# Transposing the normalised activations by DMA instead of on TensorE, and folding the rms weights into the normalisation

## Chip, core and metric

The kernel runs on one core of one Trainium2 chip. The metric is device time in microseconds of one launch. The profile is one profiled execution of the same program; its times count from the first instruction.

## What is computed

Attention with a cluster mask, followed by a gated feed-forward network (FFN), in float32 at the borders:

```python
batch, n_heads, seq, head_dim = (4, 8, 768, 64);  n_clusters = 16
n_tokens, d_model, d_ff = (3072, 512, 1536)

mask = q_assign[:, :, :, None] == k_assign[:, :, None, :]   # nearest centroid of q and of k
scores = np.where(mask, scale * np.matmul(q, k.transpose(0, 1, 3, 2)), -1e9)
attn = softmax(scores)
x = np.matmul(attn, v)        # heads side by side: 3072 x 512
rms = np.sqrt(np.mean(x * x, axis=-1, keepdims=True) + 1e-06)
xn = x / rms * rms_g
g = xn @ w_gate
val = xn @ w_val
out = (silu(g) * val) @ w_out
```

## The kernel before

**Units.** The 3072 tokens are cut into 8 units of 384 (three tiles of 128 tokens: `HT = 3`), two for each batch. For a unit, `scores` (L323) computes the masked scores of one head, with the cluster one-hot rows appended to q and k, and ScalarE takes their exponential from PSUM; `pv` (L341) multiplies by v and puts the head's normalised result into x, 128 tokens by 512 features per tile.

**From x to the FFN.** `squares` (L366) sums the squares of x; `rms` (L378) forms the inverse root with small VectorE operations and multiplies each of the three tiles by it (L386), giving xn in bf16, tokens on partitions. The FFN's matmuls contract over features, so they need xnT, features on partitions: four blocks of 128 features by 384 tokens. `xtrans` (L390) makes one such block: three TensorE transposes of 128x128 against `ident` into a PSUM tile "tx", then one VectorE instruction that multiplies by `gcol` (the rms weights, one column per block, so one scalar per partition) and writes xnT. For unit 0, `xtrans_all` (L399) does all four blocks together, with one of the four evictions on ScalarE. `gv` (L415) takes xnT as the moving operand: four matmuls for one block of 128 gate or value columns; ScalarE and VectorE make gvT of them. `out_mm` (L444) multiplies gvT by the output weights, 36 matmuls a unit in nine pieces; ScalarE copies the result to SBUF and SP stores it.

**Order.** The program is written out by hand under a manual schedule: engines work in program order, and waits follow from the tiles. `attention` (L636) goes through the 24 score steps of a unit (8 heads by 3) and puts pieces of other work behind each of them, as far as their listed costs ask. While the scores of unit u are computed, the pieces are: the last eight gate and value blocks of unit u-2, then `rms(u-1)`, then `out_mm` of unit u-2, then the first 16 gate and value blocks of unit u-1, with the preparation of a later group of heads spread among these. `CUT` marks where a unit's FFN is split between two such stretches. `border` (L532) puts the four `xtrans` of unit u-1 between the last pieces of `out_mm`. Unit 1's stretch is different: `norm` is called after the second score step (`rms(0)`, and the casts of four heads on GpSimd behind it), `xtrans_all(0)` after the sixth (`LEAD = 6`), and the first gate of unit 0 follows the seventh. After unit 7's scores come the rest of unit 6's FFN, `rms(7)`, and then unit 6's output and unit 7's FFN with nothing else between.

**Queues and buffers.** SP issues the loads of q, k and v, each waiting for a free staging buffer, and the output stores, all in program order. GpSimd issues the weight loads, which convert to bf16. x has two buffers, xn and xnT one each: xnT of a unit can be written once the unit before has had its last value matmul. The FFN's PSUM tiles, "tx" among them, rotate through three buffers. The SBUF tiles "th" of the gate pool rotate through three as well.

**The start.** `c_in`, `c_sq`, `c_n`, `ones`, `cnt` and `cntT` are small constants used in the first microseconds to build the identity and the normalised centroids; each has a place of its own. `gcol` is loaded by SP after the first loads (L569).

Of the kernel before, what the change touches and what calls it, by code (L numbers as in the profile page):

```python
# [9 lines left out]
F32 = mybir.dt.float32  # L10
BF16 = mybir.dt.bfloat16
I32 = mybir.dt.int32
AX = mybir.AxisListType.X
ALU = mybir.AluOpType
ACT = mybir.ActivationFunctionType
# [7 lines left out]
def kernel(  # L23
# [12 lines left out]
    nc = tc.nc  # L36
    B, H, S, D = q.shape
    NC = centroids.shape[1]
    DM = moe_w_gate.shape[0]
    DF = moe_w_gate.shape[1]  # L40
    P = 128
    ST = S // P
    HT = ST // 2
    UQ = HT * P
    HG = 4
    NG = B * H // HG
    UNITS = [(b, c, HT) for b in range(B) for c in (0, HT)]
    NU = len(UNITS)
    CC = DM // P
    FC = DF // P  # L50
    scale = 1.0 / (D ** 0.5)
    KR = D + NC
    WARM = 7
    CUT = CC + 2 * FC - 8
    LEAD = 6
    NQ, NV = 6, 8

# [2 lines left out]
    const = pool("const", 1)  # L60
# [4 lines left out]
    xp = pool("xp", 1)  # L65
    small = pool("small", 3)
    gate = pool("gate", 3)
# [3 lines left out]
    ps_g = pool("ps_g", 3, space=PSUM)  # L71
# [8 lines left out]
    def load(n, part, on=None):  # L80
        if n not in staged:
            staged[n] = stage.tile([P, 2, ST, D], F32, tag="qk", name="qk")
        (on or nc.sync).dma_start(out=staged[n][:, part], in_=src((q, k)[part], n))
# [9 lines left out]
        stagedv[n] = stage.tile([P, ST, D], F32, tag="vs", name="vs", bufs=NV)  # L93
        (vq or nc.sync).dma_start(out=stagedv[n], in_=src(v, n))

    c_in = const.tile([P, D], F32)
    nc.sync.dma_start(out=c_in, in_=centroids.rearrange("h c d -> (h c) d"))
    load(0, 0)
    load(0, 1, nc.scalar)
# [2 lines left out]
    for n in range(2, NQ):  # L102
        load(n, 1)
        load(n, 0)
    gcol = const.tile([P, CC], F32)


    qext = [const.tile([P, HG, S], BF16, name=f"qext{i}") for i in range(4)]
# [30 lines left out]
        return y2  # L139


    ones = const.tile([P, 32], F32)
    nc.vector.memset(ones, 1.0)
    cnt = const.tile([P, 32], F32)
    nc.vector.tensor_tensor_scan(cnt, ones, ones, 0.0, op0=ALU.mult, op1=ALU.add)
    cntT = const.tile([P, 32], F32)
    nc.vector.transpose(cntT, cnt)
    ident_f = const.tile([P, P], F32)
    nc.vector.memset(ident_f, 0.0)
    for i in range(P // 32):  # L150
        r = slice(32 * i, 32 * i + 32)
        nc.vector.tensor_tensor(ident_f[r, r], cnt[r, :], cntT[r, :], op=ALU.is_equal)
    ident = const.tile([P, P], BF16)
    nc.vector.tensor_copy(ident, ident_f)


    vbf = [const.tile([P, HG, ST, D + 1], BF16, name=f"vbf{i}") for i in range(4)]
# [5 lines left out]

    cblk = const.tile([P, H, 2 * NC], F32)
    nc.gpsimd.memset(cblk, 0.0)
    c_sq = const.tile([P, D], F32)
    c_ss = const.tile([P, 1], F32)
    nc.vector.tensor_mul(c_sq, c_in, c_in)
    nc.vector.reduce_sum(c_ss, c_sq, axis=AX)
# [3 lines left out]
    nc.scalar.activation(first_exp, off, ACT.Exp)  # L173
    c_inv = const.tile([P, 1], F32)
    nc.vector.reciprocal(c_inv, c_norm)
    c_n = const.tile([P, 2 * D], F32)
    nc.vector.tensor_scalar_mul(c_n[:, :D], c_in, c_inv)
    nc.vector.tensor_scalar_mul(c_n[:, D:], c_in, c_inv)

# [182 lines left out]
    xn = {}  # L362
# [15 lines left out]
    def rms(u):  # L378
        x, nt = xs[u], UNITS[u][2]
        for t in range(nt):  # L380
            squares(u, t, True)
        ms = small.tile([P, HT], F32, tag="ms", name="ms")
        nc.vector.scalar_tensor_tensor(ms[:, :nt], sq[u][:, 0, :nt], 1e-6, sq[u][:, 1, :nt], op0=ALU.add, op1=ALU.add)
        y = rsqrt(ms[:, :nt], nt)
        for t in range(nt):
            nc.vector.tensor_scalar_mul(xn[u][:, t], x[:, t], y[:, t:t + 1])  # L386

    xnT, gvT = {}, {}

    def xtrans(u, c):  # L390
        if c == 0:
            xnT[u] = xp.tile([P, CC, UQ], BF16, tag="xnT", name="xnT")
        ps = ps_g.tile([P, UQ], BF16, tag="gen", name="tx")
        w = UNITS[u][2] * P
        for t in range(UNITS[u][2]):
            nc.tensor.transpose(ps[:, t * P:(t + 1) * P], xn[u][:, t, c * P:(c + 1) * P], ident)  # L396
        nc.vector.tensor_scalar_mul(xnT[u][:, c, :w], ps[:, :w], gcol[:, c:c + 1])  # L397

    def xtrans_all(u):  # L399

        xnT[u] = xp.tile([P, CC, UQ], BF16, tag="xnT", name="xnT")
        ps = [ps_g.tile([P, 2, UQ], BF16, tag="gen", name="tx") for _ in range(3)]
        to = [ps[(c + 1) // 2][:, (c + 1) % 2] for c in range(CC)]
        for t in range(HT):
            for c in range(CC):
                nc.tensor.transpose(to[c][:, t * P:(t + 1) * P], xn[u][:, t, c * P:(c + 1) * P], ident)
        for c in range(CC):
            if c < CC - 1:
                nc.vector.tensor_scalar_mul(xnT[u][:, c], to[c], gcol[:, c:c + 1])
            else:  # L410
                nc.scalar.activation(xnT[u][:, c], to[c], ACT.Copy, scale=gcol[:, c:c + 1])

    gates = {}

# [29 lines left out]
    def out_mm(u, t, part):  # L444
        if part == 0:
            outs[u] = ps_g.tile([P, DM], F32, tag="gen", name="o")
        for f in range(4 * part, 4 * part + 4):
            nc.tensor.matmul(outs[u], lhsT=gvT[u][:, f, t * P:(t + 1) * P], rhs=wo[:, f], start=f == 0, stop=f == FC - 1)  # L448
        if part == 2:
            o = outp.tile([P, DM], F32, tag="o_sb", name="o_sb")  # L450
            nc.scalar.copy(o, outs[u])  # L451
            nc.sync.dma_start(out=out_rows(u, t), in_=o)
# [52 lines left out]
    def group(g):  # L505
        t, c, a = group_work(g)
        return [x for h in range(HG) for x in t[2 * h:2 * h + 2] + c[2 * h:2 * h + 2]] + a

    def spread(a, b):

        if not a:
            return list(b)
        w, n = [], 0
        for i, x in enumerate(a):
            w.append(x)
            while n < len(b) * (i + 1) // len(a):
                w.append(b[n])
                n += 1
        return w

    def ffn_work(u):
        n = UNITS[u][2] / HT
        w = [(0.18 * n, lambda c=c: xtrans(u, c)) for c in range(CC)]
        for f in range(FC):
            for val in (False, True):
                w.append((0.64 * n, lambda f=f, val=val: gv(u, f, val)))
        return w

    def out_work(u):
        return [(0.86, lambda t=t, p=p: out_mm(u, t, p)) for t in range(UNITS[u][2]) for p in range(3)]  # L530

    def border(o, ffn):  # L532

        return o[:-2] + ffn[:2] + o[-2:-1] + ffn[2:4] + o[-1:]


    def tokens(g, h, on=None):
        trans(g, h, 1, on)
# [27 lines left out]
        load_v(n)  # L566
    for n in range(H, H + HG):
        load_qk(n)
    nc.sync.dma_start(out=gcol, in_=moe_rms_g.rearrange("(c p) -> p c", p=P), allow_slow_non_contiguous=True)  # L569
    tokens(0, 2)  # L570
    casts(pool_, 2, K0, K1, Q0)
    pair_clusters(0, (1,))
# [63 lines left out]
    def attention(heads, fill, skip=0, hooks={}):  # L636
        gaps = [(u, h, i) for u, h in heads for i in range(UNITS[u][2])]
        total, done, n = sum(c for c, _ in fill), 0.0, 0
        for at, (u, h, i) in enumerate(gaps):
            scores(u, h, i)  # L640
            if i == (0 if (u, h) == (1, 0) else 1):
                for p in due:
                    pv(*p)
                due[:] = [(u, h)]
            if h == H - 1:
                squares(u, i, False)
            if (u, h, i) in hooks:
                hooks[u, h, i]()
            while n < len(fill) and at >= skip and done <= total * (at + 1 - skip) / (len(gaps) - skip):
                done += fill[n][0]  # L650
                fill[n][1]()
                n += 1
        for _, f in fill[n:]:
            f()

    attention([(0, h) for h in range(H)], [], hooks={(0, *divmod(i, HT)): f for i in range(H * HT) for f in [first.get(i, more)] if f})
    for u in range(1, NU):
        ffn, o, g = ffn_work(u - 1), out_work(u - 2) if u > 1 else [], u + 2
        if u == 1:
            t, c, a = group_work(2)  # L660
            t3, c3, a3 = group_work(3)
            n = LEAD - 4
            o3 = [(0.0, lambda i=i: load_o(i)) for i in range(0, FC, 4)]
            prep = c + a + spread(weave(t3[n:], c3), o3) + a3[:5]
            idle = const.tile([P, 1], BF16)

            def norm():
                rms(0)
                nc.gpsimd.tensor_copy(idle, xn[0][:, HT - 1, DM - 1:])
                for h in range(HG):  # L670
                    casts(pool_, H + h, K0, Q0, K1, Q1)

            hooks = {(1, 0, 0): late[6], (1, 0, 1): lambda: (late[7](), norm())}
            hooks.update({(1, *divmod(2 + i, HT)): t3[i][1] for i in range(n)})
            hooks[1, *divmod(LEAD - 1, HT)] = lambda: xtrans_all(0)
            fill = spread(ffn[CC:CUT], prep)
            attention([(1, h) for h in range(H)], fill, LEAD, hooks)
        else:
            fill = ffn_work(u - 2)[CUT:] + [(0.0, lambda u=u: rms(u - 1))]
            fill += border(spread(o[:3], [(0.0, f) for _, f in a3[5:]]) + o[3:], ffn) if u == 2 else border(o, ffn)  # L680
            attention([(u, h) for h in range(H)], fill + spread(ffn[CC:CUT], group(g) if g < NG else []), 1 if g < NG else 0)
    rest = ffn_work(NU - 2)[CUT:]
    rest[0][1]()
    pv(NU - 1, H - 1)
# [1 line left out]
        f()  # L686
    rms(NU - 1)
    nc.scalar.activation(first_exp, off, ACT.Silu)
    for _, f in border(out_work(NU - 2), ffn_work(NU - 1)) + ffn_work(NU - 1)[CC:] + out_work(NU - 1)[:-3]:
        f()  # L690
    for i in range(3):
        out_part(NU - 1, HT - 1, i)
# [30 lines left out]
```

The softmax here doesn't subtract the row's maximum and nothing guards it: scores larger than these inputs give would overflow.

## Time and profile before

| | |
|---|---|
| time, three runs | 345.44 us median (345.31 to 345.99) |
| span of the profiled execution | 343.6 us |
| median of the runs less the span | 1.84 us |
| granted TensorE clock | 1.000 |
| DMA traffic | 31.62 MB, mean 92 GB/s |
| SP load of q, 192 KB, issue to landing | median 3.9 us, 32 loads |
| SP output store, 256 KB, issue to landing | median 2.0 us, 23 stores |

The span is the time between the first and the last recorded instruction; the profile gives no other time for that execution, so the difference to the median of the runs stands for what lies around it. In the profile's rows PE is TensorE's matmul stream, PEld its weight loads, DVE VectorE, ACT ScalarE, POOL GpSimd, SP the engine that issues most DMAs; a "q" after the name is the engine's queue. A row of groups gives the line, engine, operation, output and inputs, shapes and count, then busy time and mean duration in ns, then idle time of the engine ahead of it and what ended it.

### The profile page before, as it was taken

The page shows a single profiled execution, that of the slowest core. Times are in us where ns is not written, and L with a number is a line of the kernel's source. Part 1 is how long each engine was busy: PE and PEld are TensorE (multiplying, and loading weights), DVE is VectorE, ACT ScalarE, POOL GpSimd, SP SyncE. Part 2 cuts the span into 40 slices and gives each one's busy share as a digit, 9 for nine tenths or more (in the row PEclk, how much of TensorE's full clock was granted, in tenths as well). Part 3 has the DMA queues.
Part 4 walks back from the last instruction along what each step waited for, and adds up shares of the span by engine and source line. Part 5 has one row for each costly group of instructions (what it writes and reads, how often), then busy time and mean ns, then how long its engine had stood idle before and what let it go on. Part 6 is the DMA issues. An engine that isn't in the chain of part 4 may idle for free.

```text
span 343.6 us, 8003 instructions
## 1 busy us (share of the span) xinstructions
PE 336.0 (98%) x3045; PEld 208.2 (61%) x3045; DVE 219.9 (64%) x540; ACT 259.7 (76%) x449; POOL 112.9 (33%) x225
## 2 busy tenths in 40 slices
PE   8999999999999999999999999999999999999996
PEld 3547657555766567665675656756566656655654
DVE  6999796975577626785367745686455635575330
ACT  5899979856979768786797777888688877763322
POOL 6999596234335305271131801516000000000000
PEclk9999999999999999999999999999999999999999
DMA  8999989882450015401130011000100011001002
GB/s 276 384 210 216 248 166 237 134 267 97 149 158 14 31 62 152 139 18 40 61 94 2 23 53 41 2 5 21 63 32 0 2 46 49 2 1 64 31 2 92
DMA packets 27302, 31.62 MB, mean 92 GB/s; under 512 B 4480, under 2 KB 24320, under 8 KB 27264
## 3 DMA queue, kind: packets, MB, share of 16 engines
q1 hardware_dynamic: 18608, 25.02, 22.2%
q0 software_dynamic: 8368, 5.71, 10.4%
q8 instruction: 24, 0.39, 0.5%
q10 hardware_dynamic: 288, 0.39, 0.4%
q14 instruction: 14, 0.11, 0.1%
HBM read 28.35 MB, written 6.29 MB: 101 GB/s over the span
## 4 chain that ended last, share of the span: by engine, by line
PE 82%; ACT 9%; DVE 6%; DMA 1%; issue 1%; DVEq 0%; ACTq 0%
PE o L448 17%; PE val L423 16%; PE gate L423 16%; PE s L333 15%; PE acc L351 9%; ACT pT L337 6%; PE tq L208 4%; PE sc L241 3%; PE tx L396 1%; ACT xn L376 1%; ACT th L431 1%; DVE pads L312 1%; DVE kext L317 1%; DVE qext L317 1%; DMA c_in<-in_centroids_dram 1%
## 5 line engine op out<-in xcount | busy, mean ns | idle before, releaser
L337 ACT ACTIVATE pT<-s,off 128x768 bf16<-128x768 f32 x192 | 171.3, 905 | 39.7 <-PE s L333 38.7
L333 PE MATMUL s<-qext,kext 80*128 80x384 bf16 x384 | 94.8, 327 | 2.4 <-ACT pT L337 1.6
L432 DVE SCALAR_TENSOR_TENSOR th<-th,gate 128x384 f32<-128x384 f32 x84 | 46.4, 552 | 50.8 <-ACT th L431 50.6
L423 PE MATMUL gate<-xnT,wg 128*128 128x384 bf16 x384 | 78.5, 325 | 0.1
L423 PE MATMUL val<-xnT,wv 128*128 128x384 bf16 x384 | 78.1, 326 | 0.1
L448 PE MATMUL o<-wo,gvT 128*128 128x512 bf16 x276 | 67.6, 379 | 0.0
L227 POOL CAST qext<-qkT 64x384 bf16<-64x384 f32 x64 | 35.3, 558 | 72.3 <-ACT qkT L214 63.8
L333 PEld LDWEIGHTS <-kext 80*128 80x128 bf16 x384 | 36.4, 98 | 35.1 <-issue 9.9
L436 DVE SCALAR_TENSOR_TENSOR gvT<-th,val 128x384 bf16<-128x384 f32 x84 | 46.3, 551 | 6.8 <-PE val L423 2.0
L423 PEld LDWEIGHTS <-wv 128*128 128x128 bf16 x384 | 36.3, 97 | 22.4 <-issue 0.7
L423 PEld LDWEIGHTS <-wg 128*128 128x128 bf16 x384 | 36.2, 97 | 22.0 <-issue 0.8
L351 PEld LDWEIGHTS <-pT 128*128 128x128 bf16 x1152 | 43.4, 97 | 10.1 <-DVE x L358 1.0
L431 ACT ACTIVATE th<-gate 128x384 f32<-128x384 f32 x84 | 41.3, 492 | 9.4 <-PE gate L423 8.8
L351 PE MATMUL acc<-vbf,pT 128*128 128x65 bf16 x1152 | 45.7, 193 | 0.6 <-ACT pT L337 0.2
L448 PEld LDWEIGHTS <-gvT 128*128 128x128 bf16 x276 | 25.6, 97 | 25.2 <-issue 0.6
L208 PE MATMUL tq<-ident_f,qk 128*128 128x128 f32 x192 | 30.9, 276 | 0.0
L282 POOL DMA_DIRECT2D qext<-oh x40 | 19.1, 486 | 34.7 <-DVE oh L271 28.3
L214 ACT ACTIVATE qkT<-tq 128x384 f32<-128x384 f32 x57 | 27.4, 494 | 3.4 <-PE tq L208 2.9
L397 DVE TENSOR_SCALAR xnT<-tx,gcol 128x384 bf16<-128x384 bf16 x28 | 10.4, 412 | 27.5 <-PE tx L396 27.5
L208 PEld LDWEIGHTS tq<-ident_f,qk 128*128 128x128 f32 x192 | 23.2, 141 | 6.6 <-ACT qkT L214 1.0
L451 ACT COPY o_sb<-o 128x512 f32<-128x512 f32 x23 | 13.5, 586 | 15.5 <-PE o L448 15.5
L282 POOL DMA_DIRECT2D kext<-oh x40 | 19.1, 485 | 9.6 <-DVE oh L271 9.6
(81 smaller groups left out, 246.2 us busy)
## 6 DMA issues: line engine op xcount, KB each, us to landing
qk<-in_q_dram SPq DMA_DIRECT2D x32, 192.0 KB, 3.9
vs<-in_v_dram SPq DMA_DIRECT2D x32, 192.0 KB, 4.2
out_dram<-o_sb SPq DMA_DIRECT2D x23, 256.0 KB, 2.0
qk<-in_k_dram SPq DMA_DIRECT2D x30, 192.0 KB, 3.9
wg<-in_moe_w_gate_dram POOLq DMA_DIRECT2D x4, 384.0 KB, 8.7
wv<-in_moe_w_val_dram POOLq DMA_DIRECT2D x4, 384.0 KB, 11.0
wo<-in_moe_w_out_dram POOLq DMA_DIRECT2D x3, 512.0 KB, 8.9
qext<-oh POOLq DMA_DIRECT2D x40, 12.0 KB, 1.6
```

The costliest lines, as they stand in the source:

```text
L208: nc.tensor.transpose(ps[:, i * P:(i + 1) * P], qk[:, part, 2 * i:2 * i + 2].rearrange("p t d -> p (t d)"), ident_f)
L214: nc.scalar.activation(to, ps, ACT.Copy, scale=by)
L227: on.tensor_copy(to, of)
L282: on.dma_start(out=ext[D:D + NC, h, e * UQ:(e + 1) * UQ], in_=put[g, m][32 * h + e * NC:32 * h + (e + 1) * NC])
L333: nc.tensor.matmul(ps[:, j, :w] if nt == HT else flat[:, j * w:(j + 1) * w], lhsT=cols(kext[g % 4][:KR, hh], g, kc // HT, kc % HT * P, (kc ...
L337: nc.scalar.activation(pT[u, h][:, n * i:n * i + n, :w], of, ACT.Exp, bias=off, scale=scale * ZS)
L351: nc.tensor.matmul(acc[:, h % 2, t], lhsT=pT[u, h][:, kc, t * P:(t + 1) * P], rhs=vbf[g % 4][:, hh, kc % HT * 2 + kc // HT], start=kc == 0 ...
L423: nc.tensor.matmul(ps, lhsT=w[:, c, f * P:(f + 1) * P], rhs=xnT[u][:, c, :n], start=c == 0, stop=c == CC - 1)
L431: nc.scalar.activation(th, ps, ACT.Tanh, scale=0.5)
L432: nc.vector.scalar_tensor_tensor(th, th, 1.0, ps, op0=ALU.add, op1=ALU.mult)
L436: nc.vector.scalar_tensor_tensor(gvT[u][:, f, :n], gates[u], 0.5, ps, op0=ALU.mult, op1=ALU.mult)
L448: nc.tensor.matmul(outs[u], lhsT=gvT[u][:, f, t * P:(t + 1) * P], rhs=wo[:, f], start=f == 0, stop=f == FC - 1)
```

## The change

The normalisation multiplies by the rms weights too: `grow` holds them as a row of 512 on all partitions and is the third operand. Behind the three normalisations, `rms` now calls `xtrans`, which issues three DMA transposes on SP, each from one tile of xn (128 tokens by 512 features) to the 128 token columns of all four blocks of xnT. The TensorE transposes, their PSUM tiles and evictions, `xtrans_all`, `border`, `gcol` and the bf16 identity are gone. `CUT` is four less, since the FFN's list no longer begins with four transposes; the same gate and value blocks fall on either side of it. The six small constants of the start share one buffer of the gate pool, `boot`.

```diff
-    c_in = const.tile([P, D], F32)
+    boot = gate.tile([P, UQ], F32, tag="th", name="boot")
+    c_in, c_sq, c_n = boot[:, :D], boot[:, D:2 * D], boot[:, 2 * D:4 * D]
+    ones, cnt, cntT = [boot[:, 4 * D + 32 * i:4 * D + 32 * i + 32] for i in range(3)]
...
-    gcol = const.tile([P, CC], F32)
+    grow = const.tile([P, DM], F32)
...
-    ident = const.tile([P, P], BF16)
-    nc.vector.tensor_copy(ident, ident_f)
...
         for t in range(nt):
-            nc.vector.tensor_scalar_mul(xn[u][:, t], x[:, t], y[:, t:t + 1])
+            nc.vector.scalar_tensor_tensor(xn[u][:, t], x[:, t], y[:, t:t + 1], grow, op0=ALU.mult, op1=ALU.mult)
+        xtrans(u)
...
-    def xtrans(u, c):
-        if c == 0:
-            xnT[u] = xp.tile([P, CC, UQ], BF16, tag="xnT", name="xnT")
-        ps = ps_g.tile([P, UQ], BF16, tag="gen", name="tx")
-        w = UNITS[u][2] * P
+    def xtrans(u):
+        xnT[u] = xp.tile([P, CC, UQ], BF16, tag="xnT", name="xnT")
         for t in range(UNITS[u][2]):
-            nc.tensor.transpose(ps[:, t * P:(t + 1) * P], xn[u][:, t, c * P:(c + 1) * P], ident)
-        nc.vector.tensor_scalar_mul(xnT[u][:, c, :w], ps[:, :w], gcol[:, c:c + 1])
+            nc.sync.dma_start_transpose(out=xnT[u][:, :, t * P:(t + 1) * P], in_=xn[u][:, t])
...
-        w = [(0.18 * n, lambda c=c: xtrans(u, c)) for c in range(CC)]
+        w = []
...
-    nc.sync.dma_start(out=gcol, in_=moe_rms_g.rearrange("(c p) -> p c", p=P), allow_slow_non_contiguous=True)
+    nc.sync.dma_start(out=grow, in_=moe_rms_g.unsqueeze(0).broadcast_to([P, DM]))
...
-            hooks[1, *divmod(LEAD - 1, HT)] = lambda: xtrans_all(0)
-            fill = spread(ffn[CC:CUT], prep)
+            fill = spread(ffn[:CUT], prep)
...
-            fill += border(spread(o[:3], [(0.0, f) for _, f in a3[5:]]) + o[3:], ffn) if u == 2 else border(o, ffn)
+            fill += spread(o[:3], [(0.0, f) for _, f in a3[5:]]) + o[3:] if u == 2 else o
...
-    for _, f in border(out_work(NU - 2), ffn_work(NU - 1)) + ffn_work(NU - 1)[CC:] + out_work(NU - 1)[:-3]:
+    for _, f in out_work(NU - 2) + ffn_work(NU - 1) + out_work(NU - 1)[:-3]:
```

More of the change, by code (lines that the diff above doesn't have):

```diff
@@ L53 @@
     WARM = 7
-    CUT = CC + 2 * FC - 8
+    CUT = 2 * FC - 8
     LEAD = 6
@@ L139, in rsqrt @@
         return y2
-    ones = const.tile([P, 32], F32)
     nc.vector.memset(ones, 1.0)
-    cnt = const.tile([P, 32], F32)
     nc.vector.tensor_tensor_scan(cnt, ones, ones, 0.0, op0=ALU.mult, op1=ALU.add)
-    cntT = const.tile([P, 32], F32)
     nc.vector.transpose(cntT, cnt)
@@ L165 @@
     nc.gpsimd.memset(cblk, 0.0)
-    c_sq = const.tile([P, D], F32)
     c_ss = const.tile([P, 1], F32)
@@ L175 @@
     nc.vector.reciprocal(c_inv, c_norm)
-    c_n = const.tile([P, 2 * D], F32)
     nc.vector.tensor_scalar_mul(c_n[:, :D], c_in, c_inv)
@@ L385, in rms @@
         for t in range(nt):
-            nc.vector.tensor_scalar_mul(xn[u][:, t], x[:, t], y[:, t:t + 1])
+            nc.vector.scalar_tensor_tensor(xn[u][:, t], x[:, t], y[:, t:t + 1], grow, op0=ALU.mult, op1=ALU.mult)
+        xtrans(u)
     xnT, gvT = {}, {}
-    def xtrans(u, c):
-        if c == 0:
-            xnT[u] = xp.tile([P, CC, UQ], BF16, tag="xnT", name="xnT")
-        ps = ps_g.tile([P, UQ], BF16, tag="gen", name="tx")
-        w = UNITS[u][2] * P
-        for t in range(UNITS[u][2]):
[L396 to L411, printed above, removed]
+    def xtrans(u):
+        xnT[u] = xp.tile([P, CC, UQ], BF16, tag="xnT", name="xnT")
+        for t in range(UNITS[u][2]):
+            nc.sync.dma_start_transpose(out=xnT[u][:, :, t * P:(t + 1) * P], in_=xn[u][:, t])
     gates = {}
@@ L530, in out_work @@
         return [(0.86, lambda t=t, p=p: out_mm(u, t, p)) for t in range(UNITS[u][2]) for p in range(3)]
-    def border(o, ffn):
-        return o[:-2] + ffn[:2] + o[-2:-1] + ffn[2:4] + o[-1:]
     def tokens(g, h, on=None):
@@ L679 @@
             fill = ffn_work(u - 2)[CUT:] + [(0.0, lambda u=u: rms(u - 1))]
-            fill += border(spread(o[:3], [(0.0, f) for _, f in a3[5:]]) + o[3:], ffn) if u == 2 else border(o, ffn)
-            attention([(u, h) for h in range(H)], fill + spread(ffn[CC:CUT], group(g) if g < NG else []), 1 if g < NG else 0)
+            fill += spread(o[:3], [(0.0, f) for _, f in a3[5:]]) + o[3:] if u == 2 else o
+            attention([(u, h) for h in range(H)], fill + spread(ffn[:CUT], group(g) if g < NG else []), 1 if g < NG else 0)
     rest = ffn_work(NU - 2)[CUT:]
```

## Prediction

> **What bounds the kernel now.** I read the page's busy shares first, then the chain that ended last.
>
> ```profile
> PE 336.0 (98%) x3045; PEld 208.2 (61%) x3045; DVE 219.9 (64%) x540; ACT 259.7 (76%) x449; POOL 112.9 (33%) x225
> PE 82%; ACT 9%; DVE 6%; DMA 1%; issue 1%; DVEq 0%; ACTq 0%
> ```
>
> TensorE is busy nearly always and carries 82% of the chain. A busy PE need not be at its peak, so I ask for the stretches around the change (length, then each engine's busy time and count; clock, DMA share and GB/s last), and then who PE waits for:
>
> ```profile
> 38.00:44.00 6.00, 5.87 (x71) 3.66 (x71) 3.87 (x10) 5.47 (x9) 4.46 (x11) 1.00 1.20 271
> 86.00:105.00 19.00, 19.00 (x191) 12.83 (x190) 12.01 (x28) 16.08 (x29) 6.07 (x12) 1.00 0.45 140
> PE s L333 <- ACT pT L337: 1.6, 6, 0.3
> ```
>
> From about 40 us PE has no holes: its largest wait, summed over the run, is 1.6 us. So a microsecond of PE work taken out after 40 us is a microsecond won, and a microsecond for which the in-order PE stands still is lost with nothing later to absorb it. The second thing to see is the 1.20 beside 38 to 44 us: the DMA engines are full there, with loads of v and weights.
>
> The transposes themselves, by tile and by form:
>
> ```profile
> L396 PE MATMUL tx<-ident,xn x84: 217/219/222, 83.0 to 316.1; 128*128 128x128 bf16 x84
> L397 DVE TENSOR_SCALAR xnT<-tx,gcol 128x384 bf16<-128x384 bf16 x28 | 10.4, 412 | 27.5 <-PE tx L396 27.5
> L386 DVE TENSOR_SCALAR xn<-x,n 128x512 bf16<-128x512 f32 x24 | 10.2, 483 | 0.3
> ```
>
> Last, the timeline at three unit borders (units 0, 2 and 7): from the normalisation to the first gate matmul, which needs all of xnT.
>
> ```profile
> 37.89 1.28 DVE L386 TENSOR_SCALAR xn<-x,n 128x512 bf16<-128x512 f32 x3
> 40.15 1.24 PE L423 MATMUL gate<-xnT,wg 128*128 128x384 bf16 x4
> ...
> 119.07 1.28 DVE L386 TENSOR_SCALAR xn<-x,n 128x512 bf16<-128x512 f32 x3
> 127.13 0.81 PE L423 MATMUL gate<-xnT,wg 128*128 128x384 bf16 x4
> ...
> 311.47 1.28 DVE L386 TENSOR_SCALAR xn<-x,n 128x512 bf16<-128x512 f32 x3
> 316.98 0.81 PE L423 MATMUL gate<-xnT,wg 128*128 128x384 bf16 x4
> ```
>
> The windows are 2.3, 8.1 and 5.5 us. Units 3 and 4 are as unit 2; unit 1 has 9.3, units 5 and 6 have 8.9 (the same two rows there).
>
> [...] the later of SP's loads at 35 us take 8 us and more to land where the median is 3.9. [...] the first warm matmuls (L117, 512 columns) start 0.43 us apart, the later o matmuls of that width 0.216.
>
> **The change part by part.**
>
> *PE.* 96 transposes go. In a run they advance PE by 0.34 us per six on the chain (84 of them, 14 groups: 4.76 us), and the first unit's twelve by 0.67. Together 5.4 us, all on the path. The gate could then start 0.67 us earlier at each border.
>
> *DVE and ACT.* Away go 31 evictions of 0.41 us, one ACT eviction of 0.65 and the 0.73 us ident cast. The 24 normalisations take a second SBUF tensor, grow. The nearest row is x<-acc,inv, a two-tensor op at 557 ns for 384 columns; with 128 more at its slope (557/384) about 0.7 us against 0.48, bounds 0.6 and 0.9 (L373, also two-tensor, reached 0.91 beside POOL). DVE has net 8 us less work and isn't the bound: nothing either way. Each first slice is ready 0.7 us after its normalisation starts, the third after some 1.9.
>
> *The start.* The six small constants in one gate buffer touch separate columns, and the buffer is rewritten only at the third gate: nothing, at worst 1 us if the engines were held for c_in's landing (2.4 us). grow is 256 KB read where gcol was 2 KB in 4-byte pieces that took 9.2 us to land; one load of its size, needed 20 us later. Its cost lies under the loads of that stage: nothing.
>
> *The new transfers.* Each unit issues three on SP, each waiting for its slice and for the last val matmul of the unit before (done before the normalisation). How far apart they run is the unknown. [...] The lower bound is 0.5 us, since a plain 192 KB load occupies SP for 0.33 to 0.43; [...] I take 1.4[...]. Landing after the last issue: 2.0 us, as the output stores. So xnT is complete 0.7 + 3 x 1.4 + 2.0 = 6.9 us after the normalisation starts, where the rings are free.
>
> *Units 1 to 6.* The first gate is due (window less the 0.67) at 8.6, 7.4 (three times) and 8.2 (twice). 6.9 is under each: hidden under out_work, by only 0.5 us at units 2 to 4. Behind the waiting transfers on SP stand three output stores, which lose up to 5 us; their buffers (three) are next wanted a unit later, so nobody waits.
>
> *Unit 7.* Due at 316.3; landing at 311.47 + 6.9 = 318.4. PE stands 2.1 us. [...]
>
> *Unit 0.* The gate is due at 40.15 - 0.67 = 39.5. SP reaches the transfers in time (its v loads are out by 35.7, and the q and k loads of head 14 and the blocked v load now come after). But these rows show what is ahead of them in the rings:
>
> ```profile
> vs<-in_v_dram SPq DMA_DIRECT2D x2, 192.0 KB, 8.4
> wg<-in_moe_w_gate_dram POOLq DMA_DIRECT2D x1, 384.0 KB, 12.2
> wv<-in_moe_w_val_dram POOLq DMA_DIRECT2D x1, 384.0 KB, 13.3
> qk<-in_q_dram SPq DMA_DIRECT2D x1, 192.0 KB, 8.6
> qk<-in_k_dram SPq DMA_DIRECT2D x1, 192.0 KB, 8.9
> ```
>
> The last q and k load (issued 35.77 and 36.48) landed at 44.4 and 45.4. The three transposes are as many bytes and take that place behind the v loads: 45.4, and an estimated 1.1 more for smaller pieces interleaved with the weights, 46.5. Even on free rings 38.6 + 4.2 + 2.0 = 44.8. PE stands 7.0 us; bounds 2.8 (pitch 0.5, no queue) and 11 (the weights' share doubling their time). No other PE work can slip in, since the gate stands in PE's order. [...]
>
> *Sum.* -5.4 + 7.0 + 1.7 + 2.1 = +5.4. On the profiled span of 343.6 that is 349.0; the median of the runs stands 1.84 above the span, so 350.8.
>
> **The rivals.**
>
> *A, slow transfers.* A pitch of 2.6 us [...] brings xnT after 10.5 us: stalls of 1.9 at unit 1, 3.1 three times, 2.3 twice, 5.7 at unit 7, 9 at unit 0, and cold clocks at 0 and 7 (3.4): 33.9 less 5.4, so 373.9. [...] Against: 128 KB is less than a load that lands in 2.3 us on free rings.
>
> *B, all hidden but little.* Pitch 0.5 and no queue at unit 0: stall 2.8 there, none elsewhere, no cold clock: 345.44 - 5.4 + 2.8 = 342.8. It wins where unit 0's stall stays under 5.4. Against it: the 8 to 9 us landings. A middle of A to B lands within the noise.
>
> *C, a coarse dependence at the start* (boot held as one piece) would add its 1 us to the forecast: 351.8, inside its range.
>
> **How the numbers follow.** The forecast, 346.5 to 357 with its bounds (stall at unit 0 of 4 to 11, at unit 7 of 0 to 5): 0.60. A: 0.24. B: 0.12. Even: 0.04. A run tells changes over 0.2% (0.7 us) from none. Faster 0.12, same 0.04, slower 0.84. The range 344 to 374 leaves out most of B and the upper third of A, 0.19.
>
> **What would show it.** PE's idle time before gate L423: some 7 us near 39.5, 2 us near 316, next to none at the six others. SP's transposes 1.4 us apart, landing about 8 us after issue near 40 us and 2 later. Gate matmuls at twice their spacing for some 3 us after the first stall. No tx rows; L386's successor near 0.7 us. The prediction is wrong if units 2 to 4 wait too (pitch above 1.6), or if the first stall is under 5 us.

## The result, and the profile after

The changed kernel takes 353.79 us (median of four runs, 352.84 to 354.62) against 345.47 us: 1.0235 of the time before, 95% interval 1.0215 to 1.0255, so slower by 8.3 us. The profiled spans, 352.0 and 343.6 us, differ by 8.4, so the account below is made on the spans.

First the page of the changed kernel: busy shares, chain, and the granted clock in 40 slices of 8.8 us.

```profile
PE 333.2 (95%) x2949; PEld 203.7 (58%) x2949; DVE 216.3 (61%) x508; ACT 259.5 (74%) x448; POOL 112.3 (32%) x225
PEclk9999959999999999999999999999999999999999
PE 77%; POOL 7%; DMA 6%; ACT 5%; issue 2%; DVE 2%; SPq 1%; ACTq 0%; DVEq 0%; POOLq 0%
```

PE has 96 matmuls fewer and is busy for a smaller share; DMA and GpSimd have come into the chain; one clock slice, the sixth (44 to 53 us), is low. Who PE waits for (total in us, times, longest) names the place:

```profile
PE gate L401 <- DMA xnT<-xn: 10.6, 2, 9.6
PE s L328 <- ACT pT L332: 2.3, 7, 0.7
```

Two of eight units wait for their transposed tile. PE's timeline at the first of them (unit 0) and at the other (unit 7):

```profile
40.61 0.50 PE L328 MATMUL s<-qext,kext 80*128 80x384 bf16 x2 [0.67 <-ACT pT L332]
50.69 1.44 PE L401 MATMUL gate<-xnT,wg 128*128 128x384 bf16 x4 [9.58 <-DMA xnT<-xn]
51.92 1.48 PE L401 MATMUL val<-xnT,wv 128*128 128x384 bf16 x4
...
325.38 0.81 PE L401 MATMUL gate<-xnT,wg 128*128 128x384 bf16 x4 [1.06 <-DMA xnT<-xn]
```

Four gate matmuls that took 0.81 us at the last unit take 1.44 at the first: after 9.58 idle microseconds PE runs at half clock (0.50). Two stretches (length, five engines' busy time and count, clock, DMA share, GB/s) show the stall, in which nothing but GpSimd and the DMA engines works, and the half clock behind it:

```profile
44.00:47.50 3.50, 0.00 (x0) 0.00 (x0) 0.00 (x0) 0.00 (x0) 3.28 (x8) 0.50 1.29 192
51.00:54.00 3.00, 3.00 (x13) 1.43 (x12) 1.11 (x2) 0.49 (x1) 2.11 (x4) 0.50 0.97 297
```

What the half clock cost against the kernel before is read from unit 0's second gate block, before and after:

```profile
42.77 0.81 PE L423 MATMUL gate<-xnT,wg 128*128 128x384 bf16 x4
...
54.46 0.81 PE L401 MATMUL gate<-xnT,wg 128*128 128x384 bf16 x4
```

From the first gate matmul to this one it is 2.62 us before (from 40.15) and 3.77 after (from 50.69), so about 1.2 lost. Against steps at full clock and without holes the loss would be 1.6 (the gate, value and score steps behind the stall take 3.2 us from start to start instead of 1.6), but the first gate block of the kernel before is slow too, 1.24 us.

The account: +9.6 at unit 0, +1.2 for the half clock, +1.1 at unit 7, -5.4 for the transposes that are gone: +6.5. Another 0.8 came in before 11 us; the kernel before has part of that too when it is profiled again (below). Another 0.7 is the wait in the first of the timeline's rows: the score step at 40.61 waits 0.67 us for ScalarE, where before unit 0's twelve transposes filled PE's time. Those 0.67 us of the 5.4 were not won. That makes 8.0 of the 8.4; the rest lies at units 1 to 7, where PE's order shows some 4.5 us won by the transposes that are gone, not 4.8, and 1.2 lost at unit 7's border, not 1.1.

### The profile page after: what moved, and what is told of

Its sections match the earlier page's. It is cut to its first block, busy times and chain, and to the rows that moved or that the text cites. A ratio compares the mean times of both kernels' runs of the same rounds, so it can differ in the third digit from the quotient of the medians.

```text
span 352.0 us, 7867 instructions
## 1 busy us (share of the span) xinstructions
PE 333.2 (95%) x2949; PEld 203.7 (58%) x2949; DVE 216.3 (61%) x508; ACT 259.5 (74%) x448; POOL 112.3 (32%) x225
## 4 chain that ended last, share of the span: by engine, by line
PE 77%; POOL 7%; DMA 6%; ACT 5%; issue 2%; DVE 2%; SPq 1%; ACTq 0%; DVEq 0%; POOLq 0%
PE o L426 16%; PE val L401 16%; PE gate L401 16%; PE s L328 14%; PE acc L346 8%; PE tq L203 4%; DMA xnT<-xn 3%; PE sc L236 3%; POOL kext L222 2%; POOL qext L222 2%; ACT pT L332 2%; DMA vs<-in_v_dram 2%; ACT xn L371 1%; ACT th L409 1%; POOL vbf L225 1%
## 5 line engine op out<-in xcount | busy, mean ns | idle before, releaser
L328 PEld LDWEIGHTS <-kext 80*128 80x128 bf16 x384 | 36.6, 99 | 36.2 <-issue 11.1
L401 PEld LDWEIGHTS <-wv 128*128 128x128 bf16 x384 | 36.7, 98 | 22.8 <-issue 1.2
L346 PEld LDWEIGHTS <-pT 128*128 128x128 bf16 x1152 | 43.5, 97 | 10.2 <-DVE x L353 1.0
L353 DVE TENSOR_TENSOR x<-acc,inv 128x384 f32<-128x384 f32 x32 | 17.8, 557 | 1.1
```

Source lines behind the costliest of these rows:

```text
L328: nc.tensor.matmul(ps[:, j, :w] if nt == HT else flat[:, j * w:(j + 1) * w], lhsT=cols(kext[g % 4][:KR, hh], g, kc // HT, kc % HT * P, (kc ...
L346: nc.tensor.matmul(acc[:, h % 2, t], lhsT=pT[u, h][:, kc, t * P:(t + 1) * P], rhs=vbf[g % 4][:, hh, kc % HT * 2 + kc // HT], start=kc == 0 ...
L401: nc.tensor.matmul(ps, lhsT=w[:, c, f * P:(f + 1) * P], rhs=xnT[u][:, c, :n], start=c == 0, stop=c == CC - 1)
```

## Experiments

Each is the changed kernel with one edit unless said otherwise.

### Unit 0, then units 0 and 7, transposed on TensorE

The normalisation still multiplies by the row, so the evictions are plain copies; `border` puts unit 7's four blocks between the output pieces.

```diff
         for t in range(nt):
             nc.vector.scalar_tensor_tensor(xn[u][:, t], x[:, t], y[:, t:t + 1], grow, op0=ALU.mult, op1=ALU.mult)
-        xtrans(u)
+        if u not in ON_PE:          # {0}, then {0, 7}
+            xtrans(u)
...
+            hooks[1, *divmod(LEAD - 1, HT)] = lambda: xtrans_all(0)
```

> Theory (the whole loss is unit 0: its three transfers stand behind SP's loads, then share the rings packet by packet with the weights, and PE stands 9.6 us and then runs at half clock for 3): with unit 0 transposed on TensorE and the other seven by DMA the stall and the half-clock stretch go, and what is left is 4.8 us won less 1.1 at unit 7 and some 0.5 because the slower normalisation holds unit 0's own transposes: 341.5 to 343.5 us, faster than the kernel before. Rival (the loss is spread: slower normalisations, stores held up on SP, the dearer start): 349 us or more.

> Both theories: unit 7's stall of 1.1 us goes and 0.7 us of transposes come back, so 0.2 to 0.8 us less than with unit 0 alone on TensorE. If unit 7's stall was also hiding something else that is late, no gain.

Measured: unit 0 alone 343.47 us, 0.9948 of the kernel before (interval 0.9928 to 0.9968); units 0 and 7, 342.55 us, 0.9906 (0.9891 to 0.9920). The first is at the upper end of what was expected; the second gains 0.9, a little more than the 0.2 to 0.8 foreseen. Seven of the first kernel's 22 runs lie at 345.8 to 346.6 us, which none of the experiments explains; five of the seven have a mean clock of 0.995, all other runs 0.998 or more. Taking one unit of eight off the DMA path turns 8.3 us lost into 2.4 won; the spread-out rival is out.

### Only unit 0 by DMA

`ON_PE` holds units 1 to 7.

> Only unit 0 is transposed by DMA, units 1 to 7 by TensorE between the output pieces as before. Theory: unit 0's stall and its half-clock stretch stay whole (gate at 49.5 to 51 us), the 4.8 us won at the other units are given back and unit 7's stall of 1.1 goes: 356 to 358.5 us, slower than with all eight by DMA. Rival (loss spread over the borders): 350 or less.

356.22 us, 1.0306 of the time before (1.0288 to 1.0324), within what was expected. PE's waits:

```profile
PE gate L432 <- DMA xnT<-xn: 8.7, 1, 8.7
PE s L330 <- ACT pT L334: 2.3, 7, 0.7
```

The gate is at 49.34 us (foreseen 49.5 to 51). The transfers of one unit in eight make the whole loss and more.

### What holds unit 0's transfers: weights or v loads

```diff
# weights later
-        load_gv(2)
-        load_gv(3)
+            hooks[1, *divmod(7, HT)] = lambda: (load_gv(2), load_gv(3))
...
# v loads later
-        for n in range(H, H + NV):
+        for n in range(H, H + 4):
             load_v(n)
...
                 rms(0)
+                for n in range(H + 4, H + NV):
+                    load_v(n)
```

> The last two slices of the gate and value weights are issued after unit 0's casts instead of at 33 to 36 us; nothing else. Theory (packet-by-packet sharing with the weights): the v loads ahead drain by about 40 us, the transfers run at their issue pace, 3 x 1.2 + 2.5 after 39.5: gate at 45 to 46.5 us instead of 50.7, time 348 to 350. Rival (the transfers are slow of themselves, whatever shares the rings): gate not earlier than 49.5, time 352.5 or more.

> Four of the eight v loads ahead of unit 0's transfers on SP are issued behind them. Theory: the first transposed packets go out at about 40 instead of 43.6 us, but then alternate with the weights' packets all the way (190 a us, 1,536 of them: 8 us): gate at 47.5 to 49 us, time 351 to 352.7. If the rings were shared by bytes instead of by packets: gate at 46 or earlier. Rival (slow of themselves): gate at 50 or later.

Weights later: 348.18 us, 1.0063 of before (1.0049 to 1.0078), gate at 44.64 us, even ahead of the range. V loads later: 351.80 us, 1.0162 (1.0145 to 1.0179), gate at 48.45. The DMA queues tell why. In the changed kernel, from 40 to 43 us and then from 44 to 47 us (q1 is SP's queue, q0 GpSimd's weights; packets, MB, share of 16 engines):

```profile
q0 software_dynamic: 388, 0.29, 61.0%
q1 hardware_dynamic: 384, 0.53, 57.4%
...
q0 software_dynamic: 573, 0.43, 90.6%
q1 hardware_dynamic: 587, 0.15, 37.9%
```

In both stretches the queues send packets nearly one for one (388 to 384, 573 to 587), whatever their size. While SP has v loads, its packets carry 1,536 bytes but for a few small ones (0.53 MB in 384), and it gets more bytes than the weights (0.29 MB); when its transposes come, they carry 256 bytes (0.15 MB in 587), and with half as many turns again it moves about a quarter as much. With the weights out of the way (the v loads, too, are nearly through then: 24 GB/s from 37 to 40 us), from 41 to 44 us:

```profile
q1 hardware_dynamic: 1119, 0.27, 52.3%
```

Three microseconds carry nearly twice the transposed packets, and the three transfers land 2.5 to 2.9 us after their issue instead of 8.3 to 9.3. Slow transfers in themselves are out.

The turns are not the whole of it. From 48.0 to 49.5 us of the changed kernel the weights are nearly done:

```profile
q1 hardware_dynamic: 468, 0.12, 140.9%
q0 software_dynamic: 24, 0.02, 7.2%
```

The transposes move some 310 packets a microsecond there. Without the weights they moved 476 from 40.4 to 41.0 us, some 800 a microsecond. At that pace the 468 would have taken 0.6 us and not 1.5, an estimate, so about 0.9 us of the wait at unit 0 has a cause that stays open.

The second experiment met its time for a partly different reason. In it, from 39.5 to 42.5 us:

```profile
q0 software_dynamic: 813, 0.60, 130.3%
...
q1 hardware_dynamic: 3, 0.00, 0.4%
```

The v loads ahead are gone, the first transpose was issued at 39.0, and yet next to no packet of it goes out until 43 (15 packets of SP's queue from 39.0): the weights had the engines to themselves for 4 us. From 44 to 47.5 us the engines moved 118 GB/s, where the turns of the changed kernel moved 192. So an early place on SP's queue bought less here than was thought (gate at 48.45 us), and taking the saturated weight queue away bought more (44.64). What makes a newly active queue wait those 4 us is open; without weights the first packet followed 1.3 us after the issue. Nor do the turns always come out even: in the kernel before, from 35.0 to 36.6 us, the weights sent 269 packets and SP's queue, with loads outstanding, 78.

### The constants' places and the row of weights

This kernel leaves out the multiplication by the rms weights, so that the normalisation is the old, cheaper one, and gives the start's constants places of their own.

```diff
-    boot = gate.tile([P, UQ], F32, tag="th", name="boot")
+    c_in = const.tile([P, D], F32)
...
-            nc.vector.scalar_tensor_tensor(xn[u][:, t], x[:, t], y[:, t:t + 1], grow, op0=ALU.mult, op1=ALU.mult)
+            nc.vector.tensor_scalar_mul(xn[u][:, t], x[:, t], y[:, t:t + 1])
```

> Leaves out the multiplication by the rms weights and the load of their row; the six small constants of the start have places of their own again; all transposes by DMA. If the shared buffer is what makes the start dearer: c_in lands after 2.4 us instead of 2.8 to 3.5 and the first score step is at 10.2 instead of 10.6 to 11.3 us; if it is chance, the step stays at 10.6 or later. The normalised slices are ready 0.8 us sooner: at unit 0 this wins under 0.5 us if the rings set the landing, and 0.8 if the transfers' own chain does; at unit 7 the stall of 1.1 falls to 0.3 or less. Time 351.5 to 353.

354.49 us (1.026, 1.0224 to 1.0297): a miss, no faster than the changed kernel. c_in landed after 2.5 us and the first score step still began at 10.75 us. Unit 0's slices were ready sooner and the gate came at 51.25, not earlier: the transfers' way through the DMA queues sets it, not the normalisation. Unit 7's wait fell only to 0.81:

```profile
320.99 1.28 DVE L381 TENSOR_SCALAR xn<-x,n 128x512 bf16<-128x512 f32 x3
321.60 3.81 SPq L389 DMA_TRANSPOSE xnT<-xn  x3
326.80 0.81 PE L401 MATMUL gate<-xnT,wg 128*128 128x384 bf16 x4 [0.81 <-DMA xnT<-xn]
```

The expectation counted from the third slice; but SP's three transfers follow one another from the first slice on, and that one was ready only 0.25 us sooner. The dearer normalisation costs a quarter microsecond there, not 0.8.

### How the price of a transfer grows

```diff
-            nc.sync.dma_start_transpose(out=xnT[u][:, :, t * P:(t + 1) * P], in_=xn[u][:, t])
+            for i in range(2 if u in (2, 3) else 4 if u in (4, 5) else 1):
...
+                nc.sync.dma_start_transpose(out=xnT[u][:, c, t * P:(t + 1) * P], in_=xn[u][:, t, c.start * P:c.stop * P])
```

> Unit 0 on TensorE; units 2 and 3 are moved in six transfers of 128x256, units 4 and 5 in twelve of 128x128, units 1, 6 and 7 in three of 128x512 as in the change. If a fixed part rules [...]: 0.85 to 0.95 us apart for 128x256, 0.65 to 0.75 for 128x128, so unit 4 and 5 are complete only some 10.5 us after their normalisation starts and stall 2 to 3 us each: 347 to 350 us. If the pace goes by bytes alone: 0.6 and 0.3, no stall, 343 to 344.

376.67 us (1.0868, 1.0817 to 1.092), far outside both. SP at units 1 (three transfers), 2 (six halves) and 4 (twelve quarters), and PE's first gate matmul of unit 4:

```profile
78.92 4.10 SPq L396 DMA_TRANSPOSE xnT<-xn  x3
120.58 7.62 SPq L396 DMA_TRANSPOSE xnT<-xn  x6
...
211.70 16.21 SPq L396 DMA_TRANSPOSE xnT<-xn  x12
```

```profile
225.28 0.48 PE L435 MATMUL gate<-xnT,wg 128*128 128x384 bf16 x1 [7.38 <-DMA xnT<-xn]
```

1.37, 1.27 and 1.35 us each, for 128x512, 128x256 and 128x128: the time that SP is held is per instruction, and the size does not show in it. Twelve small ones hold PE for 9.7 us in all at unit 4 and 8.2 at unit 5, six for 2.0 and 2.9 at units 2 and 3 (22.8 together), and half-clock stretches follow (mean clock 0.955). The expectation's split into a fixed part and one that grows with the size was the author's estimate, which no trace showed; the growth did not appear. The other direction, one transfer of 128x1536 per unit:

```diff
-        xnT[u] = xp.tile([P, CC, UQ], BF16, tag="xnT", name="xnT")
-        for t in range(UNITS[u][2]):
-            nc.sync.dma_start_transpose(out=xnT[u][:, :, t * P:(t + 1) * P], in_=xn[u][:, t])
+        xnT[u] = xp.tile([P, HT, CC, P], BF16, tag="xnT", name="xnT")
+        nc.sync.dma_start_transpose(out=xnT[u].rearrange("p t c k -> p (t c) k"), in_=xn[u].rearrange("p t f -> p (t f)"))
```

> All units by DMA, but one transfer of 128x1536 [...] per unit in place of three, issued when the third slice is ready; xnT is laid out by token tile for it, so the gate's moving operand is read in three pieces. If SP's price is per instruction [...]: SP is held 1.2 to 1.5 us per unit and unit 7's stall is 0 to 1.3 us; unit 0's gate stays at 50 to 51.5, because the same 1,536 packets alternate with the weights; time 352.5 to 354.5. If SP's time grows with the tiles after all [...]: unit 7 stalls 2 us or more, time 355 or more.

353.82 us (1.0202, 1.0138 to 1.0266), within what was expected for one price per instruction. The eight transfers, min, median and max ns on SP:

```profile
L388 SPq DMA_TRANSPOSE xnT<-xn x8: 1274/1442/3507, 40.6 to 322.1; - x8
```

A transfer of 128x1536 holds SP for 1.44 us at the median, near the 1.35 of 128x128. But the one transfer must wait for the third slice and lands 3.7 us after its issue, so unit 7 still waits 0.95; unit 0's gate stays at 50.44.

### The start, and the kernel before once more

> The kernel before, profiled once more. In its first profile the first score step is at 10.2 us and c_in lands after 2.4; in all eight changed kernels so far the step is at 10.5 to 11.3. If the later start belongs to the change: again 10.2 to 10.3. If it is how the first loads and the clock fall out in one execution: 10.4 or later.

Its first score step began at 10.66 us this time, its c_in landed after 2.4, and its time was 345.82. So some 0.4 of the 0.8 us at the start is how one execution falls out; the ten kernels with the change lie between 10.55 and 11.26. Whether the change has any share in the rest is not settled; the kernel with the constants apart (10.75) gives no sign that it is the shared buffer.

### The version that keeps both

Units 0 and 7 wholly the old way (scalar normalisation, weights as columns in the eviction), units 1 to 6 by DMA.

```diff
+            if u in ON_PE:          # {0, 7}
+                nc.vector.tensor_scalar_mul(xn[u][:, t], x[:, t], y[:, t:t + 1])
+            else:
                 nc.vector.scalar_tensor_tensor(xn[u][:, t], x[:, t], y[:, t:t + 1], grow, op0=ALU.mult, op1=ALU.mult)
```

> Units 0 and 7 wholly the old way (scalar normalisation, TensorE, weights as columns in the eviction), units 1 to 6 by DMA with the row; c_in in a place of its own. Against units 0 and 7 on TensorE with the row (342.6): unit 0's last slice is ready 0.8 us sooner, so 0.5 to 0.9 us less, and up to 0.4 more if c_in lands sooner: 341.3 to 342.1.

341.75 us, 0.9891 of the kernel before (0.9876 to 0.9905): 3.7 us below it, as expected, and 12.0 below the change's median. In its profile PE no longer waits for a transfer (its largest wait is again the 1.6 us for the exponentials) and busy shares and chain read as before the change:

```profile
PE 331.8 (98%) x2959; PEld 204.1 (60%) x2973; DVE 217.6 (64%) x516; ACT 259.9 (76%) x449; POOL 113.2 (33%) x225
PE 82%; ACT 8%; DVE 6%; issue 2%; DMA 1%; ACTq 0%; DVEq 0%
```

## Why the prediction was right, and where its terms were off

It forecast 350.8 us in 344 to 374, slower; measured 353.79. The places and the kind of loss were as it said: PE stands before the gate at units 0 and 7 alone, and runs at half clock after the first stall. Its sum of +5.4 against +8.3 is off in sizes, and what shares out the DMA engines at unit 0 it had wrong. That the sum came as near as it did is partly luck: unit 7 lost 1.0 less than forecast and the half clock 0.5 less, against 2.6 more at unit 0 and the 0.8 of the start.

- *PE's gain of 5.4.* Held but for unit 0's 0.67, which a wait for ScalarE took, and some 0.3 at the others. Six units by DMA should win 6 x 0.68 = 4.1 us of PE time; the mixed version wins 3.7.
- *Unit 0.* The mis-sized term: 7.0 forecast, 9.6 measured. The step that failed is "as many bytes", which gave the transposes the place and the pace of the q and k load they displace, plus an estimated 1.1. Bytes are not what the queues shared (0.43 MB of weights to 0.15 from 44 to 47 us, at 573 packets to 587). 384 KB of loads are 256 packets of 1,536 bytes, the three transposes 1,536 packets of 256; at first they went turn by turn with the weights, and they needed from 43.6 to about 50 us. Why the last of them stayed slow when the weights were nearly done is open. With the weights away the gate came at 44.64, close to the 44.8 that the prediction had for free rings.
- *Half clock.* 1.7 forecast, about 1.2 measured. The 1.7 (3.4 for two units in rival A) was the author's estimate; no trace had shown it. The kind is as forecast: the clock is at 0.50 from 43.8 us until 54.0, 3.3 us after the start of the first gate matmul. It fell 2.6 us after PE's last matmul had ended (0.67 idle us stood just before that matmul). In the two runs with weights or v loads later it fell about 1.7 and 1.8 us after, an estimate from their mean clock of 0.80 and 0.81 from 40 to 44 us. With smaller transfers a stall of 2.26 us at unit 3, with 0.62 more behind two gate matmuls, was enough: the next score step took 0.85 us, 0.49 before.
- *The pace on SP.* 1.4 forecast, 1.2 median (1,196 to 2,087 ns): near by luck. The 1.4 was the author's estimate, and so was the 2.6 of rival A: no trace had shown a DMA transpose. The runs with transfers of 128x128 to 128x1536 show one price per instruction, 1.2 to 1.4 us, whatever the size; rival A falls with that.
- *Landing.* 2.0 after the last issue ended, so 3.4 from its start; measured 2.5 from its start where the queues were free. With the faster pace this made unit 7's stall 1.1 instead of 2.1.
- *Units 1 to 6* were hidden, as forecast, with nobody waiting for the held-up stores.
- *Normalisation.* 0.7 forecast, 0.748 measured. The forecast carried it in the landing; with the cheaper one unit 7's stall is 0.25 us shorter.
- *The start* was costed at nothing and shows +0.8, about half of it chance; of rival C's coarse dependence there is no sign.
- *The range.* The forecast's own bounds (stalls of 4 to 11 and 0 to 5, half clock 1.7, less 5.4, on 345.44) sum to 345.7 and 357.7, not 346.5 and 357; the measured time is inside either.
- *Rival B* failed at the point that it named: unit 0's stall would have had to stay under 5.4.

## What to carry to other kernels

Moving a transpose from a saturated TensorE to idle DMA engines paid where the result was wanted late and the queues were quiet: six units of eight here, 3.7 us together. Where it is wanted at once, beside bulk loads, ask how many packets it is, not how many bytes (unit 0's 1,536 packets held PE for 9.6 us), and count the clock that an idle PE loses on top of the stall (0.50 here, about 1.2 us). Treat it unit by unit: the two borders with no cover keep the old way, and the mixture beats both pure forms.

## What the runs showed of the hardware that was not expected

- Two busy DMA queues sent nearly the same number of packets, whatever their size: 573 against 587 in 3 us, of 768 and 256 bytes (0.43 and 0.15 MB). It was not so in every stretch (269 against 78 in the kernel before).
- A DMA transpose held its issuing queue for 1.2 to 1.4 us, whatever its size: 1.35 and 1.32 on average for 128x128, 1.27 and 1.42 for 128x256, 1.21 at the median for 128x512 and 1.44 for 128x1536.
- A transpose that was issued while only the weights kept the engines busy sent almost no packet for 4 us (15 from 39.0 to 43.0 us); without the weights the first followed after 1.3 us. The cause is open.
- A stall of 2.26 us, with 0.62 more behind it, was enough for TensorE's half pace (score step 0.85 us, 0.49 before). With a long stall the half clock stood for 10.2 us in the changed kernel (43.8 to 54.0) and, worked out from the clock of the windows, for some 6.8 with the weights later and 10.2 with the v loads later.
